# Two more blocks of the first MLP as a pair with seven products, and the middle stage in a written order

## The chip, the cores and the metric

The kernel runs on one core of a Trainium2 chip. The metric is device time in microseconds (us) of one execution; the median of three runs of the kernel before is 1572.76 us. TensorE is called PE below, VectorE DVE, ScalarE ACT, GpSimd POOL, and SyncE, which issues nearly all DMAs, SP.

## The reference

```python
def _attn_ref(q, k, v):                       # all 8 x 8 x 576 x 64 (batch, heads, tokens, width)
    q_s = softmax of q over the width
    k_s = softmax of k over the tokens
    kv = einsum('bhsd,bhse->bhde', k_s, v)
    return einsum('bhsd,bhde->bhse', q_s, kv)

x = attn_out, tokens first                    # 4608 x 512
h = x @ w_in;  g = h * clip(h + 3, 0, 6) / 6;  x = g @ w_out      # first MLP, 512 -> 2048 -> 512
h = x @ w2_in; g = h * sigmoid(h);             out = g @ w2_out   # second MLP, same sizes
```

All in float32. (The softmaxes are written out in the reference; the two MLPs have their own weights.)

## The kernel before

The 4608 tokens are nine blocks of 512 (numbers 0 to 8). A matrix product in float32 is made as three products of a rounded upper part and a lower part (`fp32r`), so a 128x128 by 128x512 step costs three matmuls.

**First stage** (`first_block`): the attention of the first units, the loading and splitting of the first MLP's weights, and block 0 of the first MLP. **Middle stage** (`middle`): the rest of the attention, further blocks of the first MLP, and the making of weight sums for what follows. **Pair stage** (`second_mlp`): pairs of blocks, in which a 2x2 product of blocks is made with seven products instead of eight (Winograd's form of Strassen's method). A pass over a pair has 672 matmuls (336 of line 1366, 336 of line 1525); two blocks in the plain way have 2 x 16 x 24 = 768 (line 559 for `mm1`, line 634 for `mm2`). The tuple `PASSES` lists the passes: before, blocks 1 and 2 of the second MLP, then blocks 7 and 8 of the first MLP, then 3 and 4, 5 and 6, 7 and 8 of the second. Block 0 of the second MLP comes last, in the plain way. `NCL` counts the plain blocks of the first MLP: 7 before.

A unit of attention is a block and a pair of heads (36 units, number u; 28 of them in the middle). For its queries: `q_max` (DVE), `q_sub` (POOL, which writes the tile `qe`, of which there is one buffer), `q_exp` (ACT), `q_sum` (DVE), `q_eps` (POOL), `q_recip` (DVE), `q_norm` (POOL). Then the queries have to be turned. Units 0 to 8 do it on PE: `q_turn` (line 476, four transposes into a PSUM bank) and `q_copy` (ACT, line 501). Units 9 to 35 do it by `q_blocks` (DVE, line 484: 32x32 blocks), a store to DRAM (`q_store`) and a strided load (`q_load`, four DMAs). Which way is set by `DIRECT` in `middle`. At last `x_mm` (PE, line 513) and `x_upper` (ACT); units of block 4 and later are stored to DRAM (`xq`).

In the plain way a step f of a block is `mm1` (12 matmuls into a PSUM bank `h`), a gate (`relu` on ACT line 572, `times_h` on DVE line 599, `upper` on ACT line 590, `lower` on DVE line 593) and `mm2` (12 matmuls, line 634).

The middle also makes the weight sums for 16 pairs of weight rows of the second MLP (class `Parts`: `Conv` and `Split`, four sums on POOL in place, line 195, casts on ACT line 224, differences on DVE line 227, stores) and of the first MLP (class `Resident`). And it makes the first pair's operands: `first_operands` loads blocks 1 and 2 and makes sums t3, t1, t2, t4 (POOL, line 1239) and upper and lower parts of B11, B21, B22, T1 to T4 (ACT line 1300, DVE line 1310; 128x1024). T2 is made from t2, t4 from T2's source after T2's lower part is done, and B21 and T4 follow t4.

Each engine works its instructions off in the order in which they were emitted. In the middle that order comes from the class `Plan`: every job has an engine, a planned duration, a key and what it waits for; `Plan.run` plays the plan through, tries 400 variations of the keys, and emits the best order.

The pair stage then begins with product P1 of the first pair (B11's upper and lower part), P6 (T2), `mm2` of the last plain step, and P5 (T1):

```python
    KEYS = ("P1", "P5", "P6", "P2", "P7", "P3", "P4")
            for p in ("P1", "P6"):
                at[p], T = T, T + 1
        when(1.95, lambda: mm2(last))
```

Of the kernel before, what the change touches and what calls it, by code (L numbers as in the profile page):

```python
# [9 lines left out]
F32 = mybir.dt.float32  # L10
# [18 lines left out]
def efficient_attention_then_two_mlps(  # L29
# [709 lines left out]
    class Plan:  # L739
# [276 lines left out]

    def middle():

        DIRECT = 2 * NP + 1
        plan = Plan(  # L1020
            a=2, h=2, g=1, r=1, z=1, qe=0, qT=1, ke=0, mx=2, m1=1, t2k=5, raw=0, sp=3, x=1, wi=0,
            **{f"y{c}": 0 for c in range(NC)},
# [7 lines left out]
        def unit(u):  # L1030
            j, pr = divmod(u, NP)
            key = lambda r: begin[u] + r + 0.3
            old, has_k = u == NP * 2, u < NU
            if u > NP * 2 + 2:
                n_q[u] = dma(0.8, key(-3.4), lambda: load_q(u), 256, [qsub[u - 2]])
            if has_k and u > NP * 2 + 1:
                n_k[u] = dma(0.7, key(-3.5), lambda: load_k(u), 320, [ksub.get(u - 2)])
                n_v[u] = dma(1.0, key(-2.5), lambda: load_v(u), 320, [kvmm[u - 2]])
            kx = qn = None
            if not old:  # L1040
                qm = add("DVE", 0.7, key(0), lambda: q_max(u), [n_q.get(u)])
# [101 lines left out]
        for n, s in list(enumerate(steps))[NF - 1 : NCL * NF]:  # L1143
            ph, j, f = s
            g3 = g2 = None
            if n >= NF:
                m = None
# [12 lines left out]
                g3 = add("DVE", 0.7, n - 0.45, g.lower, [g2], [], ["h"])  # L1160
                plan.held |= {g0, g1, g2, g3}
# [103 lines left out]
    def first_operands():  # L1265
# [482 lines left out]
```

## Time and profile before

| what | value |
|---|---|
| median of 3 runs | 1572.76 us (1572.47 to 1573.2) |
| the profiled execution's own time | 1573.41 us |
| its span in the profile | 1571.7 us |
| PE busy | 1557.0 us (99%), 7403 matmuls |
| DVE, ACT, POOL busy | 1115.9 us (71%), 761.0 us (48%), 489.2 us (31%) |
| granted clock of PE, mean | 0.999 |
| DMA | 342.81 MB, mean 218 GB/s |

The span runs from the first instruction to the last. Busy time of PE counts overlapping matmuls as one stretch; how far apart matmuls start is read from the starts, not from the mean duration. The middle stage lies between about 140 and 718 us.

### The profile page before, as it was taken

How to read it: one execution, taken by the hardware profiler on the slowest of the kernel's cores; microseconds unless marked ns; L12 is line 12 of the kernel's file. 1: busy time of each engine (PE TensorE's matmuls, PEld its weight loads, DVE VectorE, ACT ScalarE, POOL GpSimd, SP SyncE). 2: the span in 40 equal slices, each digit the busy share in tenths (PEclk: the TensorE clock that was granted, in tenths of full speed). 3: DMA queues.
4: the chain of work that ended last, by engine and by line, in shares of the span. 5: the costliest groups of instructions: out<-in, count | busy, mean ns of one | idle time of the engine just before them, and what ended most of it. 6: DMA issues, size and time to landing. Idle time of an engine off the chain costs nothing.

```text
span 1571.7 us, 22243 instructions
## 1 busy us (share of the span) xinstructions
PE 1557.0 (99%) x7403; PEld 1272.4 (81%) x7403; DVE 1115.9 (71%) x1791; ACT 761.0 (48%) x1358; POOL 489.2 (31%) x446
## 2 busy tenths in 40 slices
PE   7999999999999999999999999999999999999999
PEld 4787878888888888888888888888888888888887
DVE  7989577776777776555689569856976797677732
ACT  6887345554555544443365236533643464345422
POOL 4334224433434335421232242234223422440000
PEclk9999999999999999999999999999999999999999
DMA  9915976776786855746566786765668875879850
GB/s 280 335 44 176 334 227 209 238 231 203 226 257 212 264 193 189 234 152 208 189 223 217 209 233 219 260 206 198 228 213 213 224 247 194 227 224 372 260 129 27
DMA packets 346226, 342.81 MB, mean 218 GB/s; under 512 B 126464, under 2 KB 252160, under 8 KB 346112
## 3 DMA queue, kind: packets, MB, share of 16 engines
q1 hardware_dynamic: 344496, 340.70, 68.3%
q8 instruction: 59, 0.97, 0.3%
q10 hardware_dynamic: 1616, 0.69, 0.2%
q14 instruction: 55, 0.45, 0.1%
HBM read 247.20 MB, written 94.11 MB: 217 GB/s over the span
## 4 chain that ended last, share of the span: by engine, by line
PE 95%; DVE 2%; ACT 1%; DMA 1%; POOL 1%; issue 0%; SPq 0%; DVEq 0%; ACTq 0%; POOLq 0%
PE pb L1366 24%; PE pb L1525 24%; PE h L559 21%; PE y L634 19%; PE y L636 3%; PE pa L513 2%; PE pa L412 1%; DVE fa L140 0%; PE pa L384 0%; DMA ahead<-in_q_dram 0%; DMA qraw<-in_q_dram 0%; DMA wi_early<-in_moe_w_in_dram 0%; PE pa L476 0%; PE busy L875 0%; PE pa L372 0%
## 5 line engine op out<-in xcount | busy, mean ns | idle before, releaser
L559 PE MATMUL h<-x,wi 128*128 128x512 f32 x1536 | 381.8, 396 | 2.0 <-POOL wi L165 0.9
L1366 PE MATMUL pb<-xo,ring 128*128 128x512 f32 x1680 | 383.0, 389 | 0.0
L1525 PE MATMUL pb<-gsp,ring 128*128 128x512 f32 x1680 | 382.4, 389 | 0.0
L1366 PEld LDWEIGHTS pb<-xo,ring 128*128 128x128 f32 x1680 | 315.3, 188 | 65.9 <-issue 0.5
L1525 PEld LDWEIGHTS pb<-gsp,ring 128*128 128x128 f32 x1680 | 315.3, 188 | 65.5
L559 PEld LDWEIGHTS h<-x,wi 128*128 128x128 f32 x1536 | 283.2, 188 | 65.2 <-POOL wi L165 1.9
L634 PE MATMUL y<-g,wo 128*128 128x512 f32 x1344 | 323.6, 390 | 0.0
L634 PEld LDWEIGHTS y<-g,wo 128*128 128x128 f32 x1344 | 251.3, 188 | 52.7
L1353 DVE TENSOR_TENSOR gsp<-g,gsp 128x512 fp32r<-128x512 f32 x240 | 184.4, 788 | 25.0 <-ACT gsp L1471 24.2
L1471 ACT CAST gsp<-g 128x512 fp32r<-128x512 f32 x240 | 143.6, 622 | 105.4 <-PE pb L1525 89.1
L599 DVE SCALAR_TENSOR_TENSOR h<-r,h 128x512 f32<-128x512 f32 x112 | 77.7, 693 | 108.4 <-ACT r L572 108.2
L572 ACT ACTIVATE r<-h 128x512 f32<-128x512 f32 x112 | 66.9, 597 | 175.1 <-PE h L559 173.2
L1353 POOL TENSOR_TENSOR xst<-xst 128x512 f32<-128x512 f32 x32 | 70.8, 2212 | 168.6 <-DVE xo L1353 84.5
L1353 DVE TENSOR_TENSOR g<-r,pb 128x512 f32<-128x512 f32 x96 | 65.7, 684 | 54.6 <-ACT r L1380 54.1
L1380 ACT ACTIVATE r<-pb 128x512 f32<-128x512 f32 x96 | 57.1, 595 | 97.2 <-DVE pb L1353 72.8
L1353 POOL TENSOR_TENSOR g<-g 128x512 f32<-128x512 f32 x40 | 53.5, 1337 | 148.6 <-DVE g L1353 123.4
L1353 POOL TENSOR_TENSOR s<-U,s 128x512 f32<-128x512 f32 x32 | 42.6, 1330 | 173.3 <-DVE U L1353 173.3
L590 ACT CAST g<-h 128x512 fp32r<-128x512 f32 x112 | 65.5, 585 | 48.8 <-DVE h L599 40.6
L593 DVE TENSOR_TENSOR g<-h,g 128x512 fp32r<-128x512 f32 x97 | 66.8, 689 | 28.6 <-ACT g L590 26.5
L1353 DVE TENSOR_TENSOR U<-pb,s 128x512 f32<-128x512 f32 x80 | 55.0, 688 | 17.0 <-PE pb L1366 12.5
L195 POOL TENSOR_TENSOR fa<-fa 128x256 f32<-128x256 f32 x64 | 49.9, 780 | 40.7 <-DVE sp L227 32.2
L1380 ACT ACTIVATE r<-s 128x512 f32<-128x512 f32 x32 | 20.2, 632 | 87.3 <-POOL s L1353 70.3
(160 smaller groups left out, 1751.4 us busy)
## 6 DMA issues: line engine op xcount, KB each, us to landing
ring<-ws SPq DMA_DIRECT2D x280, 512.0 KB, 3.9
ws<-sp SPq DMA_DIRECT2D x128, 256.0 KB, 3.2
wi_early<-in_moe_w_in_dram SPq DMA_DIRECT2D x16, 512.0 KB, 8.5
wo_early<-in_moe_w_out_dram SPq DMA_DIRECT2D x16, 512.0 KB, 9.2
wi_raw<-in_moe_w_in_dram SPq DMA_DIRECT2D x16, 512.0 KB, 4.7
ws<-w_sum SPq DMA_DIRECT2D x32, 256.0 KB, 3.1
ws<-fa SPq DMA_DIRECT2D x32, 256.0 KB, 2.8
wo_raw<-in_moe_w_out_dram SPq DMA_DIRECT2D x16, 512.0 KB, 4.4
```

The costliest lines, as they stand in the source:

```text
L195: lambda to=to, x=x, y=y, op=op: nc.gpsimd.tensor_tensor(out=at[to], in0=at[x], in1=at[y], op=op)
L559: nc.tensor.matmul(h, w[:, a, c, :], x[:, e, c, :], start=(c == 0 and n == 0), stop=(c == NC - 1 and n == 2),)
L572: nc.scalar.activation(self.r, self.h, AF.Relu, bias=3.0)
L590: nc.scalar.copy(self.g[:, 0], self.r)
L593: nc.vector.tensor_tensor(out=self.g[:, 1], in0=self.r, in1=f32(self.g[:, 0]), op=ALU.subtract)
L599: nc.vector.scalar_tensor_tensor(out=self.h, in0=self.r, scalar=6.0, in1=self.h, op0=ALU.min, op1=ALU.mult)
L634: nc.tensor.matmul(y[c], w[:, a, cs], g[:, e, :], start=st, stop=sp)
L1353: (eng or nc.vector).tensor_tensor(out=out, in0=a, in1=b, op=how)
L1366: nc.tensor.matmul(to, ws_[:, a], e[:, c], start=p in ("P1", "P6", "P5") and c == 0 and m == 0, stop=c == 1 and m == 2, skip_group_check=True,
L1380: nc.scalar.activation(r, d[b, n, key], AF.Sigmoid)
L1471: nc.scalar.copy(t[0], source(p, i))
L1525: nc.tensor.matmul(d[b, p][m], w[:, a, m * P : (m + 1) * P], t[e], start=new and i == 0 and k == 0, stop=i == NPR - 1 and k == 2, skip_gro ...
```

## The change

`NCL` becomes 5: blocks 0 to 4 of the first MLP are made in the plain way, and `PASSES` gets a second pass of the first MLP, (0, 7), behind (0, 5). The middle thus has 64 steps instead of 96, and the pair stage six passes instead of five. `DIRECT` becomes 36: the 27 units that were turned through DRAM are turned by PE, with `q_copy` on ACT. `k_max` gets a buffer of its own (`halved`) instead of one of the five `t2k` buffers, and there is one more buffer for `kv`. `Plan.run` isn't called for the middle; the 1987 jobs are emitted in the order that the string `MIDDLE` spells (two digits of base 64 for each job).

```diff
-    KVS = NP + 1
-    NCL = NB - 2
+    KVS = NP + 2
+    NCL = NB - 4
...
-    PASSES = ((1, 1), (0, NCL)) + tuple((1, j) for j in range(3, NB, 2))
+    PASSES = ((1, 1), (0, NCL), (0, NCL + 2)) + tuple((1, j) for j in range(3, NB, 2))
...
+    halved = const.tile([P, 2 * P], F32, name="halved")
...
-        m2 = tmp.tile([P, 8, D], F32, tag="t2k", name="m2")[:, 0:4]
+        m2 = halved.rearrange("p (h j d) -> p h j d", h=2, j=2)
...
-        DIRECT = 2 * NP + 1
+        DIRECT = NB * NP
...
-                qt_ = add("PE", 0.65, key(3), lambda: q_turn(u), [qn], ["a"], ["qe"])
-                ql = add("ACT", 0.62, key(3), lambda: q_copy(u), [qt_], ["qT"], ["a"])
+                qt_ = add("PE", 0.65, key(3), lambda: q_turn(u), [qn], ["a", "qT"], ["qe"])
+                ql = add("ACT", 0.62, key(3), lambda: q_copy(u), [qt_], [], ["a"])
...
-                    [kx, n_v.get(u), xmm.get(u - 1)], ["a"], ["ke"],
+                    [kx, n_v.get(u)], ["a"], ["ke"],
...
-        for fn in plan.run(0, 300e3):
+        for fn in plan.listed(listed(MIDDLE)):
             fn()
```

Spelt out, the order has these last jobs. On PE: `mm1` of the last plain step (block 4, f = 15), `x_mm` of unit 34, `mm2` of f = 13, `mm2` of f = 14; then the pair stage. On ACT after that `mm1`: `relu` of f = 15, `x_upper` of units 35 and 34, two casts of the last `Parts` (P10 and P11), `upper` of f = 15, and the upper parts of T2, B11, B22, B21, T4, T1. On DVE: `times_h` of f = 15, the two differences of the last `Parts`, `lower` of f = 15, and the lower parts of T2, B22, B21, T4, B11, T1. On POOL: the last four sums of `Parts`, t2, t4. T3 and t1 come earlier, beside the plain steps f = 8 to 12.

## Rows read from the trace of the kernel before

**Rows 1.** The page, busy time of the whole span.

```profile
PE 1557.0 (99%) x7403; PEld 1272.4 (81%) x7403; DVE 1115.9 (71%) x1791; ACT 761.0 (48%) x1358; POOL 489.2 (31%) x446
```

**Rows 2.** Busy time by stretch: first stage, middle, two halves of a pass.

```profile
core 0: us, PE busy (x) PEld busy (x) DVE busy (x) ACT busy (x) POOL busy (x), PEclk, DMA share, GB/s
28.00:140.00 112.00, 108.40 (x552) 84.48 (x548) 102.03 (x183) 95.40 (x179) 37.06 (x33) 1.00 0.53 175
...
140.00:718.00 578.00, 577.33 (x2973) 470.71 (x2972) 397.77 (x688) 279.96 (x508) 221.65 (x245) 1.00 0.70 225
...
870.00:947.00 77.00, 77.00 (x341) 63.77 (x340) 48.13 (x72) 27.26 (x49) 27.29 (x22) 1.00 0.81 221
947.00:1022.00 75.00, 75.00 (x333) 62.10 (x332) 68.91 (x97) 42.86 (x75) 22.61 (x11) 1.00 0.71 242
```

**Rows 3.** The chain of waits: start us, us, what.

```profile
165.86 2.72 PE y L634 x12
...
871.53 74.80 PE pb L1366 x330
```

**Rows 4.** PE in order of time, around the turning of one unit.

```profile
109.98 0.60 PE L476 MATMUL pa<-ident,qe 128*128 128x128 f32 x4
110.34 1.64 PE L559 MATMUL h<-x,wi 128*128 128x512 f32 x6
```

**Rows 5.** Groups by line in the middle, 140 to 718 us.

```profile
L599 DVE SCALAR_TENSOR_TENSOR h<-r,h 128x512 f32<-128x512 f32 x96 | 66.7, 694 | 107.2 <-ACT r L572 107.1
...
L593 DVE TENSOR_TENSOR g<-h,g 128x512 fp32r<-128x512 f32 x96 | 66.1, 689 | 28.4 <-ACT g L590 26.3 <-PE y L634 0.7
...
L484 DVE STREAM_TRANSPOSE qz<-qe 128x512 f32<-128x512 f32 x27 | 19.0, 704 | 0.7 <-POOL qe L468 0.7
...
L501 ACT COPY qt<-pa 128x512 f32<-128x512 f32 x1 | 0.6, 587 | 0.3 <-PE pa L476 0.3
```

**Rows 6.** Waits in the middle: us in total, times, longest us.

```profile
POOL qe L442 <- DVE qz L484: 47.6, 13, 12.4
```

**Rows 7.** PE in order of time, end of the middle.

```profile
712.71 2.89 PE L634 MATMUL y<-g,wo 128*128 128x512 f32 x12
715.44 1.02 PE L513 MATMUL pa<-qt,kv 128*128 128x512 f32 x2
715.90 3.32 PE L1366 MATMUL pb<-xo,ring 128*128 128x512 f32 x12
```

**Rows 8.** ACT in order of time, end of the middle.

```profile
712.97 0.60 ACT L572 ACTIVATE r<-h 128x512 f32<-128x512 f32 x1 [3.42 <-PE h L559]
713.47 1.04 ACT L1300 CAST xo<-xo 128x1024 fp32r<-128x1024 f32 x1
```

**Rows 9.** DVE in order of time, end of the middle.

```profile
684.88 1.23 DVE L1310 TENSOR_TENSOR xo<-spare,xo 128x1024 fp32r<-128x1024 f32 x1 [0.85 <-PE h L559]
686.03 0.69 DVE L599 SCALAR_TENSOR_TENSOR h<-r,h 128x512 f32<-128x512 f32 x1
...
715.63 1.22 DVE L1310 TENSOR_TENSOR xo<-xo 128x1024 fp32r<-128x1024 f32 x1
```

**Rows 10.** POOL in order of time, end of the middle.

```profile
665.09 2.77 POOL L1239 TENSOR_TENSOR spare<-spare,xo 128x1024 f32<-128x1024 f32 x1 [3.59 <-DVE xo L1310]
...
686.19 2.39 POOL L1239 TENSOR_TENSOR spare<-xo,spare 128x1024 f32<-128x1024 f32 x1 [14.67 <-DVE xo L1310]
```

**Rows 11.** PE in order of time, first stage, with idle time before.

```profile
17.87 0.32 PE L384 MATMUL ph<-ident,small 128*128 128x128 f32 x1 [1.02 <-DVE small L378]
18.86 0.33 PE L372 MATMUL ph<-ident,peaks 128*128 128x128 f32 x1 [0.66 <-DVE peaks L367]
```

**Rows 12.** Busy time and granted clock just after, and of the middle's first stretch.

```profile
18.95:22.36 3.41, 3.41 (x12) 2.62 (x13) 2.35 (x6) 2.55 (x5) 2.17 (x3) 0.52 1.03 377
...
140.00:227.00 87.00, 86.33 (x450) 69.47 (x449) 57.33 (x106) 36.21 (x68) 30.21 (x36) 1.00 0.89 290
```

**Rows 13.** DMA issues: out<-in, queue, count, KB each, median us to landing.

```profile
zd<-qz SPq DMA_DIRECT2D x27, 256.0 KB, 2.7
qt<-zd SPq DMA_DIRECT2D x108, 64.0 KB, 2.1
```

More of the change, by code (lines that the diff above doesn't have):

```diff
@@ L21 @@
 LOWEST = -3.4028234e38
+DIGITS = "0123456789ABCDEFGHIJKLMNOPQRSTUVWXYZabcdefghijklmnopqrstuvwxyz-_"
+MIDDLE = (
+    "KB02KCKDKEKLKM0001KNKOKVKWKX09KHKP0GKYE3KQ0AKJ0H0IKRKS03KF9j9kKTKU04KZKI9lKaKbKfKg0B9m9n9o0C050J0KCn"
+    "9rKh9p9sA8AAKc0NABKiG1KjKk060U0dACADKl0r9tEjAE0u0O0PKmAFKp0DAG079q0EKdKqKr0QKsKe089u9v9w9x0tKtKuKv0F"
+    "0LAo0e0fKz0vK-K_KwL0Aq0w0g0sKnAHAI0h0x0_KoKxL1KK9z0VArAJAs0k1bKy10L2L30y0z9yGh0M0RAtAu0W110l9-"
+    "AvAw0S0TL49_A00-"
+    "AKL7L8L9LA0m0n14A412LBLCLHA1A213L5LI0X0Y0Z0a15AxAyLDAUAV1EAzGjL6LFA51617AX1N1O0bLJLKLLAWAYAZLELGBS1P"
+    "A31819LMLRLS1c1l1QLNLOBUBVBWA-1A1BLTLU1RAaAbLPC61C1D1U1G1mLQA6BXBY1FBZBa1n1dLbLcC8LVLW1V1-"
+    "AcLdLXLZLeC9CALYCBCCCDBb1W0c0iIhBcCELfBdLgCFLlLmLnLo0j0oBeLhLi1H1I1XLa1z1J1K1L1MLjCGCHLkE4E6E7LpLvLw"
+    "Lq0p0q1SLrLs201T1_1o1p1sLxLyLzL-"
+    "M327M4CI211YL_M0E8C5E9EAKGM5EBECM6LtLu222328M124M725ALM8M929MA2jAMANAO1e26AP2C2DDR2MMDMEAQEDEEFP1t1f"
+    "ElMFC7MGARASMH1u1v2L1g1hMNMOMP2AAT2BM2MBMIMJFOMQMCEFFQ2V2W2XFRFSFTFU2EA92kAdEGMRAeFVFWFXIfH_JLEkMKMS"
+    "MTMUML2F2GMX2tMMMYMZMa2HFYMh1i2u2vFZMi2w2xMjMbMc1j3aMkMlAfMdMeMVMWEmG3EnEoEp2IEqFa1Z1aAgMfErEsEt2m1k"
+    "MmMn1q3j2-1r2O2lMo2N2n3Z2o2p2qMzM-M_AkN0EuEvAlAhN1EwMgG21wMp2r2sAm1x1yMq2JN22KG4N3N4Mt2_N73031MvN8Mr"
+    "G5G6G7G8G9N92yMxMu2zA_MsAiAj2Y2ZGAGBNANBNCNDNENHNINJNKN52PB0B22QB1B32R382c39HLB43kN6NL3233NR3bGCNF2S"
+    "2TNMNNGDGE3lNO2d3ACm2e2f2UCoCpNSNTNUNV3I2a2b3c3J3KB5B6NWNbNcNd3LNe3B3MMwNGMyCqCrNfNX34NY3PB8CsCt3C3D"
+    "B73-"
+    "3E2g2h3_NgB9NPNl2iNmNnCuNoNpBB3F3GBANQNhNqCv3Q3H3N3OJ_BCNZ3RBD3S3TBE3d3e483mNiNa3U3f3gCw3n494ABoNjNk"
+    "3h3i3o403VA7NvNw4Q4142CxNxNr3qBFBHBGNsCyBpBr3r3pBqBsBt4344Ny45NzN-N_BIBJ3s4R4B4CBuBKO0DQDSNtNu3tBvO3"
+    "O4Bf464ZBO4nO5DTDU4FO6O7ODOEOF4GO8O9BwOABgBPBi4P4HBh4IOGBjBk4oO13u4a4SDVDWDX4bON4c3vBQDY47CS4DBL4xOH"
+    "O2OBOCOIOJDZOLBM4d4T4U4VBN4q4g4W4XOOOPBlOKBmBnBx4EByBzCTCUDaDbCVB-Dc4yOQOXOY4JOROSOZOaOMOTCW4K4h4pCX"
+    "OV4LOU4z4-"
+    "CYCZCaOb4iCJJK5A4YJMJNOWOcOdOe59Oh4_525Y4e4jOiOjC2C3JOJPOkOr4f4k3w534rJQB_OlOm5X4sC4C0JROnOo4t54C1Os"
+    "4u4vOtOuOv55O_JS4wOfOgHNJT505COpOw5DCKCLCMP0CNCOP15J5BCPCQ5aOxOyHM51HO4l5KJUHPP2P35EJVP9PAPB5L5MOqOz"
+    "5NO-"
+    "5F5ZCRCbHQPCHRHSP4P5P6HTHU5v5yCcCdJWCeCfJJPD5QPJCiPKPLPM5R5G5HHVPEPFPGPbCgHW56575S5T5hIgIiP75w5i5ICj"
+    "35HX5O5PP8PcIjIkIlImCh635jCk3637585kPNPO4mHYInPdIo5UPe4M5b5cIpPH3WPPPf5V5dPQ5l5e5f5o64655WPIPgPhIqIr"
+    "3XPRCzPSPiPZPX5g5m5pPlPm5nC-"
+    "3Y66675zPnC_6I4N5xD0D1PoPv4OPT5qPwPxPyIs6APVDP6RPjPkPpPq6fD26B6C5rPYD3D4PrPsD6PzP-GiD76SGkPWD86TD9DA"
+    "DBP_GlGm6J6gD5PUPtQ3Q45-"
+    "Gn5_6D5sQ05tGoGpQ5Q66U6V6061PuQDQEDCDDPaQ1Q2DFApQFQ7QGQ8DdQ9De6HGqDE726pQAQB62GrDGDfDgDh5u6YDi3xDHDI"
+    "QH6ZDm6KDjDkQIDlQJQKDJ6a3yDK6869QC3z6L6M6NDnDpQNDoDq716bQOQP6iQLGsGtQQQX6q6OQRQSDrQTDL6hQYQZQa6P6QQU"
+    "Ds6r6EQMQV6F6WQb6sGu7BDtDvDwQW6XDMEQ6GQc6tDNQh7CDu6j746cERESETQdQeEH6kEUQiQjQkDOQrQfQl6wEVDxDyE07D6l"
+    "E1EWQs6m6nEX6o6x6y6z73QmQn7PQoQtE2EIEKEYEJELQuQgEMEx7Q6uClQpDzD-6vQvENQwQx75EOEZEaD_EyQyQ_EPR0F4Ez6-"
+    "6_R1707SR2R9R3R47E7RRARBQq7F7IEbE-E_R5RCF07677F1Fk7J7KQzQ-"
+    "F2R6F5F6EcR7EgF7RJEh7LF8RDRKF3RLR8EiF97nRM7Z7aRERFRHBRFlRGFm7b7oRTRUFA78797cRNFBFCFnROI0I2I3RVI4I5Fo"
+    "FpRPRQ6dRW7dI67pI7I8RdReRf7x7gI9Fq6eFDFrE57A7G7HRgFsFbRh7y7zRI7hRi7MRRRXRYEdRSRZEeEf7N7O7-"
+    "RaRbFERjRnRoFFRpRq7qIA7TFGJz7_IBICFKFLRcRk7UFM7V7WFH7X8AFIFJRxRyFcRrRz7YFd7e7iFe7jRsRtRuFf89827fFgFh"
+    "R-FiJ-7r7s7tR_RlRmS07k7lSD8384K0FtFuSESFSGFv8J7u7vFwGFF-F_8K8LRvK18MS1S2GGGH8XK2K3FjFxFyGIK4K57mRwS3"
+    "S48NK685GJGKSH8BSIG08YFzK7SB8QSCGO8C7w80S9S5S6SN81SO8RSJSK8DSP8E8FGLGMGNSQSRSX8hK8SY8GSZSaK9S7GP8HSS"
+    "STGQ8SS8GR8i8j8ZGSGTSUSLSM8k8T8IKAH286SVGUGV8lGXGYSbGWScSdSeSWSh8o8a8O8PSiGZGaGbGcH3SjSkH5H4H68b8cH7"
+    "H8Sr8d8eSsStSuSvH9SAGvUh8U8VSwGdSfSgSx968fHi8gHASyGwGxSlSmGy8WGzG-"
+    "8m8nUjSnS_GeGfT0UiT1T2G_H0GgHBH1T3HZ8p8qHC8vSoSpSqT4HDHEHjHlHk8rFNHm97T5T6HFHGHHHn9899HoT98s8t8u9WTA"
+    "TBTCSzS-HpHqTJHaID9A9B9CTKTLTDTEHbUkHcHdHITFHJTGHeHfTMTN9XIE9DT79E9FHgHK9YTOHrTTIF9Z9aIGUlIHHsHt9b9c"
+    "HuII87HhT8TPTHTQIM88TUTVTWTXAnHyHzIJIK9GH-TIILINTdTeTf9d9eTYItTgTRUmTZTSTaIPIO8wUn8xUpHvIQIRHwThTiIS"
+    "ITIVTnToHxTpTqTjTkIUIuIvIwIWTb8y8zTcTlJ09JIXTrTxTsTtIYIxIy9H9IIZIaTuIzI-J1TyJ2TzT-U5T_Ib9fI_JX8-"
+    "8_U0TmTvJ3U1J4J5J6BT9gTwUqU2IcJYJaJg9091J7J8U6U7UoU8UFU9U39293IdJZJ99KU4UAJbJcJAJBJCUBUDIeJdJeJfJhJD"
+    "UCJiJEJjUGUHUI9L9MUPUQUEJk9N9O94UJJFJlURJm9P9QUKULUSJn9RUMJGUZUaUbJpUcJqJr959S9TJHI1UTUUUVUWJoUdJI9h"
+    "9UJsJt9V9iUeJwJuJvUNUOJxUfUgUrUuUvUxV1V2UwU_V0JyUzU-UXUYUyUsUt"
+)
@@ L24, in f32, with listed @@
+def listed(text):
+    at = [DIGITS.index(x) for x in text]
+    return [64 * a + b for a, b in zip(at[::2], at[1::2])]
 def f32(ap):
@@ L360, in k_max @@
     def k_max(u):
-        t = kbuf[u]
-        m1 = peaks.rearrange("p (h d) -> p h d", h=2)
-        m2 = tmp.tile([P, 8, D], F32, tag="t2k", name="m2")[:, 0:4]
-        m2 = m2.rearrange("p (h a) d -> p h a d", h=2)
+        t, m1 = kbuf[u], peaks.rearrange("p (h d) -> p h d", h=2)
+        m2 = halved.rearrange("p (h j d) -> p h j d", h=2, j=2)
         nc.vector.tensor_tensor(out=m2, in0=t[:, :, 0:2, :], in1=t[:, :, 2:4, :], op=ALU.max)
@@ L820, in run, with listed @@
                     span, order, keys = end, got, tried
+            return self.listed(order)
+        def listed(self, order):
+            jobs = self.jobs
             return [jobs[i][3][0] if jobs[i][0] in ("SP", "AQ") else jobs[i][3] for i in order]
@@ L1052, in unit @@
                 km = add(
-                    "DVE", 1.1, key(0), lambda: k_max(u), [n_k.get(u)], ["m1", "t2k"], ["t2k"], True
+                    "DVE", 1.1, key(0), lambda: k_max(u), [n_k.get(u)], ["m1"]
                 )
@@ L1069, in unit @@
                     "PE", 0.48, key(4), lambda: kv_mm(u, a_pool),
-                    [kx, n_v.get(u), xmm.get(u - 1)], ["a"], ["ke"],
+                    [kx, n_v.get(u)], ["a"], ["ke"],
                 )
-                va = add("DVE", 0.45, key(4), lambda: kv_sum(u), [mm])
-                vlow[u] = add("ACT", 0.55, key(4), lambda: kv_scale(u), [va], [], ["a"])
+                va = add("DVE", 0.45, key(4), lambda: kv_sum(u), [mm, vlow.get(u - 2)])
+                vlow[u] = add("ACT", 0.55, key(4), lambda: kv_scale(u), [va, xmm.get(u - KVS + NP)], [], ["a"])
             xm = xmm[u] = add(
@@ L1146, in middle @@
             if n >= NF:
-                m = None
+                m = free.get(n - 1)
                 for c in range(NC):
@@ L1288, in first_operands @@
         for n, name in enumerate(("B22", "B11", "B21")):
-            jobs.append((name.lower(), "SP", 0.35, 2.5 + n, load(name), 512, ("r1",), ["wi"], False))
+            jobs.append((name.lower(), "SP", 0.35, 2.5 + n, load(name), 512, ("r1", "b12"), ["wi"], False))
         def total(name, key, deps):
```

## The prediction

> **What bounds the kernel now.** I read the page first, for the engines' shares: PE is busy 99% of the span, no other engine over 71% [rows 1]. Then the busy time by stretch, to see whether that holds in the stage that changes: in the middle PE is busy 577.3 of 578 us and DVE 397.8, so there is work for PE at every moment and DVE has 180 us to spare [rows 2]. Then the chain of waits, for what a busy PE costs: 12 plain matmuls take 2.72 us and 330 matmuls of a pass 74.80 us, both 0.2267 us each [rows 3]. So the time is the sum of what PE is given, plus whatever new wait the other engines bring.
>
> All sums are made against the profiled execution's 1573.41 us (span 1571.7 and 1.7 around it); the median shown is 0.65 lower, which is taken off at the end.
>
> **Matmuls.** Two plain blocks go, 768 matmuls; a pass comes, 672. That is 96 x 0.2267 = **-21.8 us**. Passes run without a pause even where DVE is busy 69 of 75 us [rows 2], so the sixth pass gets the same price.
>
> **Turning by PE.** 27 units get four transposes each. In the first stage the matmul behind the four starts 0.36 us after the first of them [rows 4]. 27 x 0.36 = **+9.7 us**, all on the path, since PE has no gap to put them in. ACT gets 27 copies of 0.59, DVE loses 27 block transposes of 0.70 [rows 5], and SP loses 27 stores and 108 loads [rows 13]. What speaks for a higher price is a rival below.
>
> **The other engines in a shorter middle.** It becomes 578 - 174.1 + 9.7 = 414 us (two blocks are 768 x 0.2267 = 174.1). DVE loses 32 steps of 0.694 + 0.689 and the 27 transposes [rows 5]: 397.8 - 44.3 - 19.0 = 334.5, 81% of it instead of 69%. ACT and POOL stay lower. DMA moved 225 GB/s x 578 us = 130 MB [rows 2]; less 27 x 0.51 MB for the queries' way through DRAM [rows 13] it is 116 MB in 414 us, 280 GB/s. The middle's first stretch did 290 GB/s at 0.89 without a loss on PE [rows 12]. So nothing becomes the bound by its sum, but covers get thinner. The trace of before can't show what waits that makes. From below: none, as in the middle and in the passes' second halves (DVE at 92%). From above: the first stage, where DVE was at 91% and PE idle 3.6 of 112 us [rows 2], which is 13.3 in 414. A gain isn't possible, as PE had no idle time to give back. I went through the written order for the loops with one other engine (a PE job, the work of DVE or ACT behind it up to what PE next needs, against PE's own work between): they come out between even and a few us to spare, so I take **+1.0 us**, near the lower end, and keep 13.3.
>
> **The end of the middle.** Here the written order puts the first pair's operands last. In the kernel before, B22's lower part ended at 716.85, just after the pass had begun at 715.90 [rows 7, 9]. Counted from the end of the last `mm1` (the start of PE's next instruction):
> - ACT starts `relu` 0.26 later (712.71 to 712.97) and the next instruction 0.50 behind it [rows 7, 8]. Five things stand between `relu` and T2's upper part (two `x_upper`, two casts, `upper`): that begins at 0.26 + 6 x 0.50 = 3.3 and takes 1.04, to 4.3.
> - T2's lower part on DVE takes 1.23 [rows 9]: 5.5. POOL begins 0.08 later (686.11 to 686.19) and t4 takes 2.39 [rows 9, 10]: 8.0. t2 (2.77) and the four sums before it are done by then, as they hang on steps before the last.
> - B21's upper part, 1.04 and a handoff of 0.1: 9.1; its lower part 1.23: 10.3. Behind it on DVE stand T4's and then B11's lower parts; such instructions start 1.15 apart (684.88 to 686.03) [rows 9]: B11's ends at 12.6.
>
> P1, the first product of the pass, needs B11's lower part in its second matmul. PE has till then `x_mm` of unit 34 (0.46, from 715.44 to 715.90 [rows 7]), two `mm2` of 2.72 and one matmul: 6.1 us. `mm2` of the last step stands behind P1 and P6 in PE's queue, so it can't fill the gap; nothing else is queued. **+6.5 us**, with 5.5 and 7.5 as ends for ten handoffs of 0.1 either way. T1, done 1.15 later, isn't waited for, since P1 and P6 take 2.7 us. The ring's next fetches stand on SP behind the last store of the weight sums, some 3 us after the last `mm1`; they have until the sixth product and cost nothing.
>
> **The clock after that wait.** In the first stage PE was idle 1.02 and 0.66 us within 2 us [rows 11], and right after that the granted clock was 0.52 on the mean for 3.41 us, its lower level of 1.2 GHz [rows 12]. A wait of 6.5 us should bring that as well: half of 3.41, **+1.7 us**, with ends of 0 and 3.4. The Trainium skill (TensorE: Matmul & The Clock Gate, Part 1) says the same of an idle PE, that it goes back to half rate until activity lifts it again.
>
> **Sum.** 1573.41 - 21.8 + 9.7 + 1.0 + 6.5 + 1.7 = 1570.5; less 0.65 for the median, **1569.9 us**. That is 0.18% under 1572.76, and about 0.2% (3.1 us) is what a measurement of this kernel can tell from no change.
>
> **The edits costed at nothing.** `halved` takes `k_max` out of the five `t2k` buffers, and the sixth `kv` buffer lets `kv_mm` go without waiting for `x_mm`: both only loosen, in a stage where PE had no idle time. Without them DVE or PE would wait for a buffer for a unit's length.
>
> **Rivals.**
> 1. *The end isn't waited for.* If the chain at the end is shorter than I read it (ACT ahead of the casts, B11 not last), terms of 6.5 and 1.7 fall away: 1573.41 - 21.8 + 9.7 + 1.0 - 0.65 = 1561.7. For it: in the kernel before the same chain was never waited for. Against: each step of it hangs on the last `mm1`, which no engine can get ahead of. Chance 0.20, faster.
> 2. *PE waits for the queries.* There is one `qe` buffer. Before, it was released by DVE, and POOL waited for that 47.6 us in all at `q_sub` [rows 6], which PE never felt. Now PE's `q_turn` releases it and also waits for `q_norm` on POOL, behind sums of weights. Each lateness of `q_norm` is PE's wait then. It would decide from 6.0 / 27 = 0.22 us per unit on, where 1569.9 passes 1575.9; at 0.5 us it is 1569.9 - 1.0 + 13.5 = 1582.4, about the first stage's rate. For it: POOL's four sums stand in front of many `q_norm`. Against: POOL is busy 54% of the shorter middle (221.7 of 414 [rows 2]). Chance 0.18, nearly all slower.
> 3. *Transposes don't overlap.* A transpose costs its whole duration instead of a quarter of 0.36. The longest sum from rows is the 0.60 us of the four, from first start to last end [rows 4]: 27 x 0.24 = 6.5 more, 1576.4. Against: the next matmul did start at 0.36. Chance 0.04, slower. The Trainium skill (TensorE: Matmul & The Clock Gate, Part 4) gives about 275 ns for one in a kernel; at 4 x 0.275 for each unit the change would come to about 1590. By that rule the start at 0.36 couldn't be; the trace does not agree.
>
> **How the numbers follow.** The forecast has 0.58. Within it, a clock that stays up (1568.2) or a middle with no wait at all (1568.9) is faster by over 0.2% (under 1569.6): 0.20 of the 0.58; the other 0.38 are within. With rival 1: faster 0.40. Rival 2 gives 0.16 to slower (over 1575.9) and 0.02 to same, rival 3 0.04 to slower: same 0.40, slower 0.20. The range goes from rival 1 with no wait (1561) to between the decision point and the price of rival 2 (1579); the forecast's own is 1567 to 1574.
>
> **What would show it.** Right: some 3 us or less of idle PE inside the middle; 27 more groups of line 476 with 0.36 to the next matmul; then PE idle 6 to 7 us at the first product of the pass, released by DVE line 1310, with the granted clock at half behind it; and a sixth pass of 152.3 us. Wrong: no such gap; a wait at line 476 on POOL line 468 in most units; a gap between the two passes of the first MLP; or PE's matmuls further apart than 0.2267 in the middle.

## The result and the profile after

The changed kernel takes **1582.31 us** (median of 4 runs, 1581.38 to 1582.83) where the kernel before takes 1572.74 beside it: a ratio of 1.006 with a 95% interval of 1.0042 to 1.0077, slower by over 0.2%. 1569.9 was forecast. Its profiled execution took 1581.38 us (span 1579.7), 8.0 more than the 1573.41 of before.

Line numbers in the kernel after: `mm1` L615, `mm2` L690, `q_turn` L532, `q_copy` L557, `q_norm` L524, `k_max` L421 to L423, `k_turn` L428, `k_peak` L434, `k_spread` L440, the gate's `times_h` L655 and `lower` L649, `Split`'s upper and lower part L282 and L285, the weights' `shift` (DVE) L191, POOL's sums L253 and L330 and its `q_sub` L498, `q_max` L490, `x_mm` L569, `kv_mm` L468, the gate's `upper` L646, the sums t1 to t4 L1299, the pair's operands L1360 (upper) and L1370 (lower), the products L1426 and L1585.

First the busy time by stretch, as in [rows 2]: first stage, middle, first pass, and 6.82 us in which the clock was low.

```profile
core 0: us, PE busy (x) PEld busy (x) DVE busy (x) ACT busy (x) POOL busy (x), PEclk, DMA share, GB/s
28.00:135.00 107.00, 103.78 (x525) 80.90 (x524) 96.96 (x172) 91.16 (x170) 34.93 (x31) 1.00 0.55 182
135.00:563.00 428.00, 422.11 (x2321) 337.53 (x2321) 347.12 (x589) 247.79 (x461) 229.59 (x245) 1.00 0.82 262
567.47:574.29 6.82, 4.16 (x10) 3.30 (x11) 3.74 (x4) 0.73 (x2) 0.00 (x0) 0.50 0.35 134
563.00:716.00 153.00, 146.28 (x637) 120.75 (x637) 117.60 (x167) 74.64 (x126) 40.82 (x25) 0.98 0.63 210
```

The middle, in which PE was busy all but 0.7 of 578 us, now leaves PE idle 5.9 of 428. DVE is at 347 us, 12.6 over the 334.5 that the prediction worked out. The first pass begins with a long pause. It stands in the order of time of PE (start, us, ..., idle time before):

```profile
556.56 1.02 PE L569 MATMUL pa<-qt,kv 128*128 128x512 f32 x2
557.02 6.04 PE L690 MATMUL y<-g,wo 128*128 128x512 f32 x24
562.91 0.50 PE L1426 MATMUL pb<-xo,ring 128*128 128x512 f32 x1
570.13 2.50 PE L1426 MATMUL pb<-xo,ring 128*128 128x512 f32 x5 [6.72 <-DVE xo L1370]
```

From there on nothing is lost. In the chain of waits the passes run as in [rows 3], 152.32 us from one to the next (727.16 to 879.48):

```profile
727.16 74.80 PE pb L1426 x330
...
804.68 74.80 PE pb L1585 x330
879.48 74.80 PE pb L1426 x330
```

What PE waited for inside the middle, 135 to 562 us (us in total, times, longest us):

```profile
PE h L615 <- DVE g L649: 2.5, 2, 1.6
PE pa L440 <- DVE small L434: 1.9, 4, 0.8
PE pa L428 <- DVE peaks L423: 0.6, 1, 0.6
PE pa L569 <- ACT qt L557: 0.6, 1, 0.6
PE y L690 <- ACT g L646: 0.4, 1, 0.4
```

5.0 of these 6.0 us are DVE's: a bank of `h` that `lower` hasn't read yet, and the keys' maximum. POOL's `q_norm` isn't there.

**The account** by starts of PE's instructions, profiled execution against profiled execution. The prediction's terms for matmuls and turnings make the middle, from the first `mm2` of step 15 of block 0 to the first product, 576.5 + 2.7 (what moved over the border) - 174.1 + 9.7 = 414.8 us; it took 427.3, **12.5 more**. The passes with their first wait took 925.7 where 917.1 (before's 764.75 for five passes and 152.32) was to be had without one, **8.6 more**. The first stage was 1.1 shorter. 1573.41 - 21.8 + 9.7 + 12.5 + 8.6 - 1.1 = 1581.3.

### The profile page after: what moved, and what is told of

Its sections match the earlier page's. It is cut to its first block, busy times and chain, and to the rows that moved or that the text cites. A ratio compares the mean times of both kernels' runs of the same rounds, so it can differ in the third digit from the quotient of the medians.

```text
span 1579.7 us, 22420 instructions
## 1 busy us (share of the span) xinstructions
PE 1554.8 (98%) x7415; PEld 1265.6 (80%) x7415; DVE 1180.6 (75%) x1849; ACT 798.9 (51%) x1433; POOL 549.6 (35%) x478
## 4 chain that ended last, share of the span: by engine, by line
PE 64%; DVE 0%; ACT 0%; issue 0%; DVEq 0%
PE pb L1426 29%; PE pb L1585 29%; PE h L615 3%; PE y L692 3%; PE y L728 0%; PE y L690 0%; DVE xo L1370 0%; DVE o L733 0%; ACT o L733 0%; DVEq L733 0%
## 5 line engine op out<-in xcount | busy, mean ns | idle before, releaser
L1426 PE MATMUL pb<-xo,ring 128*128 128x512 f32 x2016 | 461.4, 391 | 6.7 <-DVE xo L1370 6.7
L1585 PE MATMUL pb<-gsp,ring 128*128 128x512 f32 x2016 | 458.9, 389 | 0.0
L1426 PEld LDWEIGHTS pb<-xo,ring 128*128 128x128 f32 x2016 | 379.8, 188 | 86.2 <-DVE xo L1370 7.0
L1585 PEld LDWEIGHTS pb<-gsp,ring 128*128 128x128 f32 x2016 | 378.5, 188 | 78.5
L615 PE MATMUL h<-x,wi 128*128 128x512 f32 x1152 | 293.8, 398 | 4.4 <-DVE g L649 2.5
L615 PEld LDWEIGHTS h<-x,wi 128*128 128x128 f32 x1152 | 210.7, 188 | 51.9 <-DVE g L649 5.0
L690 PE MATMUL y<-g,wo 128*128 128x512 f32 x960 | 240.2, 397 | 0.4 <-ACT g L646 0.4
L690 PEld LDWEIGHTS y<-g,wo 128*128 128x128 f32 x960 | 177.3, 188 | 40.1 <-issue 1.9
L646 ACT CAST g<-h 128x512 fp32r<-128x512 f32 x80 | 46.8, 586 | 60.8 <-DVE h L655 52.7
L1413 POOL TENSOR_TENSOR spare<-g,g 128x512 f32<-128x512 f32 x48 | 64.0, 1333 | 3.8
L655 DVE SCALAR_TENSOR_TENSOR h<-r,h 128x512 f32<-128x512 f32 x80 | 54.9, 687 | 13.5 <-ACT r L628 13.4
L498 POOL TENSOR_TENSOR qe<-qraw,qm 128x512 f32<-128x512 f32 x34 | 39.9, 1173 | 62.8 <-PE pa L532 35.3
```

What stands on the lines that cost most here:

```text
L498: eng.tensor_tensor(out=e.rearrange("p i h d -> p h i d"), in0=qt.pop(u), in1=live.pop(("qm", u)).to_broadcast([P, 2, NCH, D]), op=ALU.sub ...
L615: nc.tensor.matmul(h, w[:, a, c, :], x[:, e, c, :], start=(c == 0 and n == 0), stop=(c == NC - 1 and n == 2),)
L646: nc.scalar.copy(self.g[:, 0], self.r)
L655: nc.vector.scalar_tensor_tensor(out=self.h, in0=self.r, scalar=6.0, in1=self.h, op0=ALU.min, op1=ALU.mult)
L690: nc.tensor.matmul(y[c], w[:, a, cs], g[:, e, :], start=st, stop=sp)
L1413: (eng or nc.vector).tensor_tensor(out=out, in0=a, in1=b, op=how)
```

## The experiments

All are measured beside the kernel before (1572.5 to 1572.9 in these runs). e2 is an edit of the kernel before, all others are edits of the kernel after. The theory behind them, formed from the two traces: the 8.6 is the chain that ends in B11, as predicted; the 12.5 is DVE being late, because its instructions with both operands in SBUF take longer beside POOL's, and a dearer turning.

### e1_tail: the pair's operands in another order

```diff
+    MOVES = ((1979, 1985), (1980, 1986), (1974, 1985), (1975, 1986))   # B11 and T1, upper and lower,
+                                                                       # ahead of B22's
...
-        for fn in plan.listed(listed(MIDDLE)):
+        for fn in plan.listed(moved(listed(MIDDLE))):
```

> The changed kernel, with one thing altered: at the end of the middle the upper and lower parts of B11 and T1 are made right behind T2's, ahead of B22, B21 and T4, on ACT and on DVE. Theory (the wait of 6.7 us at the pass's first product is the order of DVE's last jobs): B11's lower part ends about 6.7 us after the last mm1 instead of 12.6, PE has 6.1 us of own work, so the wait falls to 0.5 to 1 us and the half clock behind it goes as well: 6 + 2 = 8 us less, about 1574. Rival (the end is bound by POOL's sums or by casts, whatever the order): the wait stays over 4 us, and the time over 1578.

1575.26 us (1574.7 to 1575.7), 7.0 less than after. The passes took 918.0 us instead of 925.7, the middle 1.4 more, and the clock stayed up:

```profile
564.00:574.00 10.00, 9.04 (x40) 7.05 (x39) 10.00 (x8) 5.89 (x8) 3.32 (x1) 1.00 0.89 312
```

So the wait was B11's place in the order and nothing it depends on; what stands behind P1 (B22, t4, B21, T4) isn't late when it comes.

### e2_turn: the turning alone, in the kernel before

```diff
-        DIRECT = 2 * NP + 1
+        DIRECT = NB * NP
...
-                qt_ = add("PE", 0.65, key(3), lambda: q_turn(u), [qn], ["a"], ["qe"])
-                ql = add("ACT", 0.62, key(3), lambda: q_copy(u), [qt_], ["qT"], ["a"])
+                qt_ = add("PE", 0.65, key(3), lambda: q_turn(u), [qn], ["a", "qT"], ["qe"])
+                ql = add("ACT", 0.62, key(3), lambda: q_copy(u), [qt_], [], ["a"])
```

> The kernel before, with the queries of all units turned by PE, and nothing else of the change (seven plain blocks, order from the plan's own search). It measures the price of 27 turns in a middle that has time to spare. By the predicted price of 0.36 us each: 1572.7 + 9.7 = 1582.4. With the delay of some 0.1 us that the trace of the changed kernel shows at the second matmul behind a group of small ones: 27 x 0.46 = 12.4, 1585. If PE also waits at line 476 for POOL's q_norm (the rival of the prediction): 1590 and more.

1588.38 us (1588.04 to 1589.29): 15.8 more than before, 0.59 for each turning. By the starts of PE's instructions, 10.3 of it is the 27 groups of four transposes (0.38 each), 1.4 is 15 more places (81 instead of 66) at which a large matmul behind a group of small ones comes late, and 2.9 is three waits; the last 1 is spread over pauses too short to list. PE's waits in e2's middle, 138 to 730 us (one of 0.2 is left out):

```profile
PE pa L476 <- issue: 1.2, 1, 1.2
PE pa L476 <- POOL qe L468: 1.0, 1, 1.0
PE pa L513 <- ACT qt L501: 0.7, 1, 0.7
```

Without these three a turning costs 0.48: of the expectation's prices 0.36 was too low and 0.46 nearly right. A wait for `q_norm` came once (L468, at 652 us), not at every turning. Those late matmuls can be seen at any turning, here in the kernel after:

```profile
284.89 0.60 PE L532 MATMUL pa<-ident,qe 128*128 128x128 f32 x4
285.24 2.33 PE L615 MATMUL h<-x,wi 128*128 128x512 f32 x9
287.50 0.80 PE L468 MATMUL pa<-vbuf,ke 128*64 128x65 f32 x20
```

The nine matmuls of L615 hold PE from 285.24 to 287.50, 2.26 us, where nine at 0.2267 are 2.04. By their starts, the first holds PE 0.32 us and the last, ahead of K times V, 0.32; the seven between 0.23 each. A long first one stands behind every group of small matmuls: 66 times in before's middle and 94 times in after's, 0.094 us over 0.2267 on the mean. The long last one is rarer; over all groups of after it is 0.02. A turning thus costs 0.389 (its four, up to the next start) + 0.094 + 0.02 = **0.50 us**, not 0.36.

### e3_pool_light: POOL's sums made short

```diff
-                out=at[to], in0=at[x], in1=at[y], op=op
+                out=at[to][:, 0:32], in0=at[x][:, 0:32], in1=at[y][:, 0:32], op=op
```

> The changed kernel, with POOL's sums of weights in place made on 32 of 256 columns (128 instructions of 0.82 us become short; the sums are thereby left out for the other columns). DVE's work is untouched. Theory A (DVE's instructions with both operands in SBUF take up to twice as long beside POOL's, so DVE comes late and PE waits for it): DVE's excess in the middle falls from 65 us to under 45, the waits of PE inside the middle from about 9 us to under 4, and the time by 4 to 7 us, to 1575 to 1578. Theory B (DMAs are late) and theory C (DVE has too much work of its own): within 1.5 us of 1582.3.

1577.10 us (1575.68 to 1578.0). POOL's 128 sums fall from 0.82 to 0.32 us; DVE, which does the same work as in after, is busy 19 us less, and PE's listed waits fall from 6.0 to 3.3 us:

```profile
135.00:563.00 428.00, 421.33 (x2325) 338.13 (x2323) 328.19 (x591) 250.27 (x464) 163.70 (x247) 1.00 0.82 265
```

```profile
PE h L615 <- DVE g L649: 2.4, 3, 1.7
PE y L690 <- ACT g L646: 0.5, 1, 0.5
PE pa L440 <- DVE small L434: 0.4, 1, 0.4
```

The stretching itself is plain in after, from 135 to 563 us (ns: shortest, median, longest). Above, two instructions with two operands in SBUF and one with a single operand there and a constant (L191); then one with one operand of the two in PSUM, and a reduce:

```profile
L422 DVE TENSOR_TENSOR peaks<-halved x23: 291/710/1262, 140.2 to 474.2; 128x128 f32<-128x128 f32 x23
L285 DVE TENSOR_TENSOR sp<-fa,sp x32: 634/693/2885, 150.5 to 551.8; 128x512 fp32r<-128x512 f32 x32
L191 DVE TENSOR_SCALAR fa<-fa x32: 374/432/1270, 145.4 to 548.1; 128x512 uint32<-128x512 uint32 x32
L649 DVE TENSOR_TENSOR g<-h,g x64: 637/685/694, 144.8 to 561.0; 128x512 fp32r<-128x512 f32 x64
L490 DVE TENSOR_REDUCE qm<-qraw x27: 633/676/682, 138.5 to 543.0; 128x8 f32<-128x512 f32 x27
```

By the trace, L422 took 0.29 us nine times, with no instruction of POOL beside it, and 0.70 to 1.26 us fourteen times, each time behind one of POOL that had begun before it, and it ended some 0.15 us after that one. So what lengthens it is that it waits for POOL's instruction to end.

And here is one case of what it does, DVE, POOL and PE in order of time, ahead of PE's longest wait:

```profile
331.74 1.02 DVE L422 TENSOR_TENSOR peaks<-halved 128x128 f32<-128x128 f32 x1
332.79 1.27 DVE L423 TENSOR_TENSOR peaks<-peaks,kbuf 128x128 f32<-128x128 f32 x1
333.98 1.77 DVE L285 TENSOR_TENSOR sp<-fa,sp 128x512 fp32r<-128x512 f32 x1
...
336.26 0.67 DVE L649 TENSOR_TENSOR g<-h,g 128x512 fp32r<-128x512 f32 x1
```

```profile
331.44 1.17 POOL L498 TENSOR_TENSOR qe<-qraw,qm 128x512 f32<-128x512 f32 x1 [3.19 <-PE pa L532]
332.57 2.63 POOL L330 TENSOR_TENSOR w_sum<-wo 128x512 f32<-128x512 f32 x2
```

```profile
336.99 1.19 PE L615 MATMUL h<-x,wi 128*128 128x512 f32 x4 [1.64 <-DVE g L649]
```

Three instructions of DVE take 4.06 us there that take 0.29 + 0.29 + 0.69 = 1.27 with POOL silent. The gate's `lower`, which releases the bank of `h`, stands behind them. The instructions of POOL beside them are `q_sub` (L498) and L330, not the sums (L253) that e3 makes short: e3 has this wait still, with 1.7 us.

### e4_dma_double and e6_dma_light: are transfers late?

```diff
 e4
-                dma(0.7, at + 3 + n, lambda w=w, n=n: w.store(n), 384)
+                dma(0.7, at + 3 + n, lambda w=w, n=n: (w.store(n), w.store(n)), 384)
 e6
-                n_k[u] = dma(0.7, key(-3.5), lambda: load_k(u), 320, [ksub.get(u - 2)])
-                n_v[u] = dma(1.0, key(-2.5), lambda: load_v(u), 320, [kvmm[u - 2]])
+                n_k[u] = dma(0.7, key(-3.5), lambda: kbuf.update({u: kbuf[u % 2]}), 320, [ksub.get(u - 2)])
+                n_v[u] = dma(1.0, key(-2.5), lambda: vbuf.update({u: vbuf[u % 2]}), 320, [kvmm[u - 2]])
```

> The changed kernel, with the 48 stores of the first MLP's split weights issued twice: 12.6 MB more in the middle, about 11% of its bytes. Theory B (the middle is late because its DMAs are): each 10% of bytes costs several us, 1586 or more. Theory A (DVE beside POOL): nothing hangs on these stores, within 1.5 us of 1582.3.

> After, with the loads of K and V of the middle's units left out (the units compute on what the two buffers held before, so the output is not the attention's): 24 x 640 KB, some 15 MB of the 112 that the middle moves at 263 GB/s. e4 showed that 12.6 MB more cost 34 us, with the SP queue waiting for its own transfers 74 us. A (in the kernel after itself the transfers are in time, and VectorE is what is late): within 1.5 us of 1582.3. C (transfers are a part of what is late in after): the middle gives back 2 us or more, 1580 or less.

e4 took 1616.69 us. That lies in theory B's "1586 or more", but not for B's reason. Its SP queue shows why (waits from 134 to 596 us):

```profile
SPq L265 <- DMA ws<-wi: 45.0, 17, 5.6
SPq L265 <- DMA ws<-wo: 36.1, 16, 4.7
```

The second store of the same rows waits until the first has landed, 81 us in all, and every load queued behind it on SP comes late. It is the program that makes it wait: SP has 42 semaphore waits at L265 in e4's middle and 2 in after's. So e4 measures a queue that stands still, not the price of 12.6 MB. The reading of it that stands in e6's expectation, that these are transfers which wait for each other's bandwidth, doesn't hold; in the kernel after, SP never waits at L265 for a store. e6 settles it for the loads of K and V: with 229 GB/s instead of 262 (share 0.69 instead of 0.82) it took 1583.52 us, 1.2 *more* than after. A lack of bandwidth isn't what PE waits for.

### e5_kmax_reduce: the keys' maximum as one reduce

```diff
-        nc.vector.tensor_tensor(out=m2, in0=t[:, :, 0:2, :], in1=t[:, :, 2:4, :], op=ALU.max)
-        nc.vector.tensor_tensor(out=m1, in0=m2[:, :, 0, :], in1=m2[:, :, 1, :], op=ALU.max)
-        nc.vector.tensor_tensor(out=m1, in0=m1, in1=t[:, :, KCH, :], op=ALU.max)
+        nc.vector.tensor_reduce(
+            out=m1, in_=t.rearrange("p h j d -> p h d j"), op=ALU.max, axis=AX.X
+        )
```

> After, with the maximum over the keys' five chunks as one tensor_reduce instead of three tensor_tensor. In after the three take 41.5 us for 23 units of the middle (14.2 + 14.8 + 12.5), 1.8 us each; a reduce of 512 elements takes 0.675 us there and does not lengthen beside POOL, so one of 640 is taken at 0.84, 19 in all: VectorE loses 22 us of its 346. A (TensorE's new waits come from VectorE being late, and VectorE is late because its instructions with both operands in SBUF lengthen beside POOL): the waits at the turning of the maxima and at their spreading go, and some of those for a bank of h; 1577 to 1580. B (the waits come from the order the jobs are written in, whatever the jobs last): within 1.2 us of the kernel after, 1581.1 to 1583.5.

1576.97 us (1576.8 to 1578.49), 5.3 less than after and 0.03 under A's 1577. The reduce takes 1.31 us, not 0.84, always the same:

```profile
L420 DVE TENSOR_REDUCE peaks<-kbuf x23: 1275/1310/1340, 141.0 to 468.5; 128x128 f32<-128x640 f32 x23
```

That is more than the three take with POOL silent (0.42 + 0.29 + 0.29 = 1.0), and 0.5 us under their mean of 1.80. PE's waits in the middle shrink from 6.0 to 1.6 us (lines are one lower here):

```profile
PE pa L439 <- DVE small L433: 0.8, 3, 0.4
PE h L614 <- DVE g L648: 0.6, 2, 0.4
PE pa L568 <- ACT qt L556: 0.2, 1, 0.2
```

### e11_light_kmax: e3 and e5 together

> e3 and e5 together, on the kernel after: POOL's sums on 32 of 256 columns (the output leaves the rest of the sums out) and one reduce for the keys' maximum. What is then left of the middle over the 414.8 us that the prediction's terms give should be the price of the turnings alone, 27 x (0.389 + 0.094 + 0.02 - 0.36) = 3.9 us, with waits of TensorE at or under 1 us. A: a middle of 418.3 to 420.5 us, the wait of 6.7 us at its end unchanged, and a time of 1572.8 to 1575. B (something besides VectorE's lateness holds TensorE in the middle): 421.5 or more, as e5 alone has 422.0 and e3 alone 423.0.

The middle took 419.7 us, as A has it, and what is left over 414.8 is the turning's 3.9 and 1.0 more. The waits listed come to 0.8. The time was 1575.23 us (1574.22 to 1577.35), 0.2 above A's upper end; its profiled execution took 1575.4.

### e7_plan_order and e12_plan_as_before: the planner's order instead of the written one

```diff
-        for fn in plan.listed(listed(MIDDLE)):
+        for fn in plan.run():                     # e7; e12: plan.run(0, 300e3)
```

> After, with the middle's order searched by the planner from the jobs' keys, needs and costs (which gives VectorE's and POOL's SBUF instructions one port, and lets two of them not run at once) instead of the written order. A: as the planner keeps them apart, the excess of VectorE's SBUF instructions over their shortest falls from 65 us, and TensorE's waits in the middle to under 5; the wait at the end of the middle can come out anywhere from 0 to 9; 1573 to 1581. B (the written order is the better one, and the keys don't fit these shorter blocks): over 1584.

> e7 once more, with the planner called as the kernel before calls it (no variations, transfers planned at 300 GB/s), where e7 had 400 variations and 235 GB/s, less than the 262 GB/s that the middle moves. If e7's 1670 came from planning with too slow transfers, this one is near the kernel after, 1575 to 1600. If it came from keys that fit a middle of 578 us and not one of 427, TensorE waits for q_norm at the end of the middle here too, and it takes over 1630.

1670.36 and 1659.41 us, the second theory in both. (The 400 variations and 235 GB/s of e7 are the function's defaults; before calls it as e12 does, so that before's order is the plan's first one, without variations.) With the planner's port most instructions on DVE stretch less: L422 takes 0.406 us on the mean in e12 and 0.643 in after (L198 takes longer, 0.963 and 0.771). But up to 500 us PE is busy, and then the attention that was put off comes all at once. e12 from 500 to 640 us, busy time and the largest of PE's waits:

```profile
500.00:640.00 140.00, 79.67 (x404) 55.87 (x402) 84.43 (x144) 65.22 (x118) 74.55 (x83) 0.70 0.64 204
```

```profile
PE pa L532 <- POOL qe L524: 36.9, 7, 11.2
```

So with these keys the shorter middle needs another order, and the written one is worth 77 us against the planner's. Here also is the wait of rival 2, at `q_turn` on `q_norm`; the written order keeps clear of it.

### e8_tail_kmax, e9_fewer_groups, e10_nine_groups: e1 and e5 together, then groups side by side

e8 is e1 and e5 together. e9 and e10 add pairs to `MOVES` that put a group of small matmuls beside another one:

```diff
+        (146, 116), (238, 194), (170, 1512), (1532, 245), (316, 275), (366, 350),
+        (414, 1669), (398, 1698), (618, 577))             # e10; e9 has (347, 326) and (462, 1729) too
```

> e1 (the border's parts ahead, 1575.3) and e5 (one reduce for the keys' maximum) together. A: the two mechanisms lie in different stretches and add: 1575.3 less what e5 gains on 1582.3, so 1570 to 1573.5. B: 1574.5 to 1576.

> e8 (1569.3) with eleven of TensorE's jobs of the middle moved past one to three neighbours, so that eleven groups of small matmuls (a turning, the maxima's transposes, K times V, queries times KV) stand right beside another group: 91 groups instead of 102, the same instructions. In the traces of before, after, e2 and e8 the first 512-column matmul behind a group of small ones takes 0.090 to 0.098 us longer from start to start, 66 times in before's middle and 94 times in after's. A (the price belongs to a change from small to large matmuls): 11 x 0.094, 1.0 us less, 1567.6 to 1569.0, and 83 such places in the trace instead of 94. B (the price belongs to the small instructions themselves, however they are grouped): 1568.8 to 1570.

> e9 without two of its eleven moves: the spreading of unit 27's maxima right behind unit 26's queries times KV, where TensorE waited 1.6 us for a PSUM bank that ScalarE was still copying from, and unit 22's K times V, behind whose old place a wait of 0.7 us for a bank of h came to light. If grouping saves 0.094 us for each group and e9 lost it to those two waits, the middle comes to 422.1 or 422.2 us, against 423.0 in e8 and 424.2 in e9, and the whole to 1568.3 to 1569.5 where e8 has 1569.3. If delays of single jobs of TensorE cost as much elsewhere, the middle stays at 423 or above.

e8: **1569.31 us** (1568.51 to 1571.03), a ratio to before of 0.998 (0.9971 to 0.999), so it is faster than both kernels: 13.0 under after, where e1 gave 7.0 and e5 5.3 (A's lower end was 1570). e9: 1571.34 us, over both of its expectations. It has 84 places with a long first matmul behind a group (A had said 83), but PE waited anew, at a maxima's spreading put ahead of nine matmuls, for a PSUM bank:

```profile
415.18 0.32 PE L439 MATMUL pa<-ident,small 128*128 128x128 f32 x1 [1.62 <-ACT xq L578]
```

e10, without the two moves that did harm: **1568.68 us** (1568.07 to 1570.48), ratio 0.9977 (0.9968 to 0.9987), with a middle of 421.4 us (422.1 was expected) and 86 such places. That is 0.6 under e8, measured beside other runs, and less than what can be told apart. The places are counted in the traces; that the time follows their number is not shown by e9 and e10.

## Why the prediction was wrong

**Matmuls, -21.8: right.** Six passes of 152.32 us, the sixth at the price of the others.

**The end of the middle, +6.5: right in size, one link of it by luck; +1.7 for the clock: right.** PE waited 6.72 us, for DVE's L1370; by the starts, the second matmul of the pass came 6.6 later behind the first than in before. Behind it the clock stood at 0.50 from 567.47 to 574.29; PE had 4.16 us of work in that time, and lost 2.0 by it. Together 8.6 by the starts, where 8.2 was said. e1 takes both away by reordering four jobs. Rival 1 is dead.

The chain itself differs from the forecast in two links. ACT's last `upper` (L646) stood 0.95 us waiting for an `mm2` (L690), so T2's upper part began 4.3 us after the last `mm1` instead of 3.3. And B21's upper part didn't wait for t4 at all. ACT, POOL and DVE in order of time:

```profile
560.37 0.59 ACT L646 CAST g<-h 128x512 fp32r<-128x512 f32 x1 [0.95 <-PE y L690]
561.81 2.94 ACT L1360 CAST xo<-xo 128x1024 fp32r<-128x1024 f32 x3
563.24 2.34 POOL L1299 TENSOR_TENSOR spare<-xo,spare 128x1024 f32<-128x1024 f32 x1 [4.30 <-DVE xo L1370]
563.83 2.83 DVE L1370 TENSOR_TENSOR xo<-xo 128x1024 fp32r<-128x1024 f32 x1 [0.67 <-ACT xo L1360]
```

The upper parts of B11, B22 and B21 were done at 564.75, and t4 at 565.58. What held DVE was B22's lower part, which took 2.83 us beside t4 instead of 1.21 and ended 1.1 us behind it. The forecast had 1.04 and 0.1 in that place, for B21's upper part; that the two are equally long is luck. B11's lower part ended 13.5 us after the last `mm1` instead of 12.6, and PE's own work lasted 6.6 instead of 6.1.

**Turning by PE, +9.7: too low by 3.9.** The step that failed took the price up to the start of the next matmul. The rest stood in [rows 4]: the six matmuls behind the turning take 1.64 us, where six without a pause are 5 x 0.2267 + 0.39 (the mean of one record) = 1.52 from the first start to the last end. A group of small matmuls is paid for in the first large matmul behind it too. Rival 3 is dead as well: the four start 0.11 apart, and the next matmul 0.03 after the last. The 275 ns of the Trainium skill (TensorE: Matmul & The Clock Gate, Part 4) is what one record lasts here (ns: shortest, median, longest), not what one more costs:

```profile
L532 PE MATMUL pa<-ident,qe x112: 270/273/330, 139.8 to 553.7; 128*128 128x128 f32 x112
```

**The other engines in a shorter middle, +1.0: this is the step that failed**, with 8.6 (12.5 less 3.9), inside its bounds of 0 and 13.3. The sentence "nothing becomes the bound by its sum" was true. What was wrong was to work out DVE's sum and the loops with before's durations as if they belonged to the instructions. POOL's share went from 38% to 54%, and those instructions of DVE that lengthen beside POOL's grew with it: `k_max` from 1.40 to 1.80 us, the three forms of L285 from 0.76 to 0.85, L191 from 0.55 to 0.62. One of the three of `k_max`, in before and in after (us in total, mean ns):

```profile
L366 DVE TENSOR_TENSOR peaks<-m 128x128 f32<-128x128 f32 x23 | 9.9, 433 | 0.8
L422 DVE TENSOR_TENSOR peaks<-halved 128x128 f32<-128x128 f32 x23 | 14.8, 643 | 0.9
```

Its shortest is 291 ns in both, so before's trace had the lengthening already. DVE's excess over the shortest of each kind went from 44 us to 65 in a middle three quarters as long, 8 of the 65 at L191. In the loops that "come out between even and a few us to spare", PE waited most for `lower` and `k_peak` (4.4 of the 6.0 us). These don't stretch themselves, but they share DVE with those that do, and a `lower` or a `k_peak` behind three long ones is PE's wait. Of the middle's 12.5 us e3 (POOL shortened) gave back 4.3, e5 (an instruction that doesn't stretch) 5.3 and e11 (both) 7.6, and e6 rules out the loads of K and V.

The Trainium skill (SBUF — State Buffer, Who interferes with whom) has the rule that the prediction left out: a DVE instruction with two SBUF inputs contends with a GpSimd instruction that reads SBUF, one with a single SBUF input doesn't unless it runs in a 2-port mode, which `tensor_scalar` can enter, and a reduce never does. The rows shown under e3 agree: L422 and L285 lengthen, L649 (longest 694 ns) and L490 (682) don't, and L191, a `tensor_scalar`, does (1270); which mode it ran in, no run shows. It also says that the loser blocks for the whole instruction of the other. The longest lower part of `Split` (L285) shows just that, POOL's line first:

```profile
517.30 2.87 POOL L1299 TENSOR_TENSOR spare<-xo,spare 128x1024 f32<-128x1024 f32 x1
```

```profile
517.83 2.88 DVE L285 TENSOR_TENSOR sp<-fa,sp 128x512 fp32r<-128x512 f32 x1
```

It is put off until POOL's instruction ends at 520.17, and ends 0.54 later.

**Rival 2** had the price (1582.4) and the wrong mechanism: PE waited for `q_norm` 0.2 us in all, and that at a weight load. Its place exists, though. It costs 1.0 us in e2, and 31 and 37 in the planner's order with the shorter middle (e7, e12).

**The median**: 0.65 was taken off for the profiled execution; it was 0.93 under its median instead.

What stays open: of the 8.6, the view of waits lists 6.0, of which 1.0 is put down to ACT; the rest is in pauses too short for it, and is put down to DVE only because e11 gives back 7.6 of the 12.5.

## What to carry to other kernels

A duration read from a trace holds for the neighbours it had there: before a stage is compressed, split DVE's instructions into those that lengthen beside POOL's (two SBUF operands, and here also the `tensor_scalar` of L191 with one) and the rest, and price the first by their long values where POOL's share rises. Read what a small group of matmuls costs up to the *second* large matmul behind it. And in a written order, look first at what the next stage's first instruction needs: four jobs in another order were worth 7 us.

## What the hardware showed that was not expected

- A reduce over a view with the reduced axis 64 elements apart took 1.31 us for 640 elements (2.05 ns each), where one over adjacent elements takes 0.676 for 512 (1.32 ns each). The first also writes 128 results and the second 8; which of the two makes the difference isn't shown.
- Behind a group of small float32 matmuls (128 columns, or 65) the first large one holds PE 0.31 to 0.34 us instead of 0.2267, whichever the group: 0.090 to 0.098 us more on the mean in each of the traces in which it was counted (66 times in before's middle, 94 in after's).
- PE's last work ended at 563.4; the granted clock fell to 0.50 (1.2 GHz) at 567.47, inside the wait, and was up again at 574.29, 4.16 us after PE had gone on.
